# Moving x's block sums into the first MLP, emptying GpSimd in the second, and reordering VectorE and ScalarE within a pair

## The chip, the core and the metric

The kernel runs on one core of a Trainium2 chip. TensorE (PE) does the matrix products and writes PSUM; VectorE (DVE), ScalarE (ACT) and GpSimd (POOL) do the elementwise work; SyncE (SP) issues the DMAs between HBM and SBUF. Each engine works off its own queue in the order written and waits on semaphores of the others. The metric is the device time of one execution in microseconds. Before the change it is 1678.28 us, the median of three runs (1677.06 to 1678.48).

## The reference

Three stages run one after the other: an attention whose keys and values are first packed to 32 rows per head, an MLP with ELU, and an MLP with a rational activation. Everything is float32.

```python
p_packed = sm_attn(p, k, v)                    # 8 x 8 heads, 32 packed rows
out = sm_attn(q, p_packed, p_packed)           # 576 rows a head
x = out.transpose(0, 2, 1, 3).reshape(4608, 512)
h = x @ w_in;  x = where(h > 0, h, exp(min(h, 0)) - 1) @ w_out       # 512 -> 2048 -> 512
h = x @ w_in2
P = a[0] + a[1]*h + a[2]*h**2 + a[3]*h**3
Q = 1 + abs(b[0])*abs(h) + abs(b[1])*h**2
return (P / (Q + 1e-6)) @ w_out2
```

The inputs are scaled so that h is large, and the products need nearly full float32 precision. So every operand of a product is split into a high part (a cast to fp32r) and a low part (the value less its high part), and each product is three matmuls: high by high, high by low, low by high.

## The kernel before

**First MLP.** The attention of batch element b+1 and the first MLP of element b run interleaved, in 256 steps: 8 batch elements, 2 halves of 288 tokens, 16 tiles of 128 hidden features (`a_step`, L361). Step s issues six matmuls that make h of step s+2 (L382), ACT's exp and relu (L391, L392) and DVE's maximum (L397) for s+2, the high part on ACT (L402) and the low part on DVE (L407) for s+1, and twelve matmuls that add step s to the output in PSUM (L417). What else belongs to a step stands in four tables keyed by step: `ldq` (loads, run first), `peq` (attention matmuls), `cvq`, and `ewq` (other elementwise work, run after the step's own, L1222). At the end of a half, `a_evac` copies x, [128, 4, 288], from PSUM to SBUF, and `a_spill` (L447) writes it to the HBM tensor x2d with one DMA.

**Second MLP.** x @ w_in2 is done by the Strassen-Winograd scheme: x and w_in2 are cut into 2 by 2 blocks, and seven block products P1 to P7 replace eight. x's blocks are: two halves of the contraction by the two token halves of a batch element. Of x, the seven left operands are four blocks and four sums (t1 to t4), each with a high and a low part. The 2304 token columns are cut into 6 blocks of 384 (`TU`), the 16 hidden tiles into 8 pairs: 48 pairs in all. Per block, `x_load` brings x into two staging tiles, POOL makes the sums (`x_t`, L666), ACT the high parts (`x_hi`, L655) and POOL the low parts (`x_lo`, L660), during the pairs of the block before (for block 0, during the last steps of the first MLP).

Per pair and tile f (1 and 0) the activation is worked out from h: ACT makes Abs, Square and Identity (L701, L704, L707), DVE makes Q (L711) and two products `ta`, `tb` (L715, L719), ACT Ln and Exp (L722, L725) for the reciprocal, DVE two Newton steps `Na`, `Nb` (L729) and the result g (L733), ACT g's high part (L743), POOL its low part (L746). The second product takes 36 matmuls of 512 columns a pair (`out_mm`, L754) into six PSUM tiles, which are copied out at the end of each block (`out_ev`, L771).

**Order of a pair.** `window(s)` (L777) writes the three pairs in flight by hand: the products of pair s+2, the activation of s+1, the output of s. TensorE's order is P1, o0, P2, o1, P6, o2, P5, P7, o3, o4, P4, o5, P3, where P is six matmuls of 384 columns and o six of 512. All seven products go through one PSUM tile, `ab`, with two banks. Readers of it are ACT's copies s1, u2, u3 (`keep`, L692) and C21 (L867), and DVE's additions C12, C11, C22 (`c_add`, L695). The program orders every use of this tile behind the one written before it, on whichever engine and in whichever bank: P1, C12, s1, P2, C11, P6, u2, P5, P7, u3, C22, P4, C21, P3. Fourteen yields of windows -2 and -1 are pumped into the last steps of the first MLP (L1223).

Of the kernel before, what the change touches and what calls it, by code (L numbers as in the profile page):

```python
# [22 lines left out]
def packed_attention_moe_moe2_kernel(  # L23
# [399 lines left out]
    def a_evac(s):  # L423

        b, n, f, _ = a_step(s)
        if b == 0 and f < NF - 1:
# [3 lines left out]
        elif b == 0 and n == 1:  # L430
            x = mlp["x", s] = part[0][:, 1]
        elif b == B - 1:
            if n == 0:
                part[:] = [P.tile([128, 2, NKD, TA], F32, tag="v", name="xlast")]
            x = mlp["x", s] = part[0][:, n]
# [177 lines left out]
    P1, P2, P6, P5, P7, P4, P3 = range(7)  # L613

    swt, wo2, xs, stg, bst = {}, {}, [], {}, {}

    def s_load(p):
        for t in range(4):
            n = 2 if t < 3 else 1
            w = P.tile([128, n, 2, 2, 128], F32R, tag=f"wo{4 * (p % 2) + t}", name=f"sw_{p}_{t}")  # L620
            nc.sync.dma_start(out=w.bitcast(F32), in_=s2d[:, p % NPR, 2 * t:2 * t + n].bitcast(F32))
            swt[p, t] = w
# [11 lines left out]
    def x_slots(i):
        if i == 0:
            t = P.tile([128, 5, 2, 2, TU], F32R, tag="wi", name="xs_wi")
            xs.extend(t[:, k] for k in range(5))
        else:
            xs.append(P.tile([128, 2, 2, TU], F32R, tag=f"m{i - 1}", name=f"xs_m{i - 1}"))

    def x_stage():
        for tag in "kq":
            stg[tag] = P.tile([128, 3, 2, TU], F32, tag=tag, name=f"stage_{tag}")

    def x_load(n):
        u = slice(n * TU, (n + 1) * TU)
        for tag, k in (("k", 0), ("q", 2)):
            for i in range(2):
                nc.sync.dma_start(out=stg[tag][:, i], in_=x2d[:, k:k + 2, i, u])

    XSRC = (("k", 0), ("q", 0), ("k", 0), ("k", 2), ("k", 1), ("q", 0), ("q", 1))

    def x_hi(n, j):
        tag, i = XSRC[j]
        nc.scalar.copy(xslot(n, j)[:, 0], stg[tag][:, i])  # L655

    def x_lo(n, j):
        tag, i = XSRC[j]
        x = xslot(n, j)
        nc.gpsimd.tensor_tensor(x[:, 1], stg[tag][:, i], x[:, 0].bitcast(F32), ALU.subtract)  # L660

    def x_t(i):
        k, q = stg["k"], stg["q"]
        o, a, b = ((k[:, 2], k[:, 1], k[:, 0]), (k[:, 0], q[:, 1], k[:, 2]),
                   (k[:, 1], q[:, 1], k[:, 1]), (q[:, 0], q[:, 0], k[:, 0]))[i]
        nc.gpsimd.tensor_tensor(o, a, b, ALU.subtract)  # L666
# [623 lines left out]
```

## Time and profile before

| | |
|---|---|
| Median of three runs | 1678.28 us |
| Profiled execution | 1679.38 us |
| Its span, first to last instruction | 1677.6 us |
| TensorE busy | 1519.9 us (91%) |
| VectorE busy | 1226.6 us (73%) |
| ScalarE busy | 1080.7 us (64%) |
| GpSimd busy | 320.0 us (19%) |
| Mean granted clock of TensorE | 0.982 of full speed |
| Moved by DMA | 253.88 MB, 151 GB/s |

The time of the profiled execution is its span and 1.78 us around it. Busy time is the time in which an engine had an instruction running. TensorE's matmuls overlap and the ends of them are modelled, so the distance from one start to the next tells its pace, not the duration. The same holds for DVE and ACT in a smaller way: an instruction can start some hundredths of a microsecond before the one ahead of it is recorded as done. Two stages have to be kept apart: up to 717.1 us the first MLP alone, from 759.34 us the pairs of the second alone, with a mixture between.

### The profile page before, as it was taken

The page shows a single profiled execution, that of the slowest core. Times are in us where ns is not written, and L with a number is a line of the kernel's source. Part 1 is how long each engine was busy: PE and PEld are TensorE (multiplying, and loading weights), DVE is VectorE, ACT ScalarE, POOL GpSimd, SP SyncE. Part 2 cuts the span into 40 slices and gives each one's busy share as a digit, 9 for nine tenths or more (in the row PEclk, how much of TensorE's full clock was granted, in tenths as well). Part 3 has the DMA queues.
Part 4 walks back from the last instruction along what each step waited for, and adds up shares of the span by engine and source line. Part 5 has one row for each costly group of instructions (what it writes and reads, how often), then busy time and mean ns, then how long its engine had stood idle before and what let it go on. Part 6 is the DMA issues. An engine that isn't in the chain of part 4 may idle for free.

```text
span 1677.6 us, 26163 instructions
## 1 busy us (share of the span) xinstructions
PE 1519.9 (91%) x10194; PEld 1339.4 (80%) x10194; DVE 1226.6 (73%) x1826; ACT 1080.7 (64%) x1902; POOL 320.0 (19%) x170
## 2 busy tenths in 40 slices
PE   7899999999999999989888987888888888888987
PEld 5789899999999899987767866777777777777776
DVE  6886767666666667657777778677777787877776
ACT  4866666667676766566666666666656756665664
POOL 0000000000000000412442235233413432342221
PEclk9999999999999999999999999999999999999999
DMA  9533344444444323255544644654454446444531
GB/s 355 166 118 132 96 133 127 125 129 125 137 142 148 120 95 130 71 181 190 169 148 161 206 143 138 221 173 147 156 199 149 149 159 222 153 138 164 173 128 38
DMA packets 116490, 253.88 MB, mean 151 GB/s; under 512 B 9488, under 2 KB 55824, under 8 KB 114576
## 3 DMA queue, kind: packets, MB, share of 16 engines
q1 hardware_dynamic: 116368, 252.22, 46.0%
q8 instruction: 80, 1.31, 0.3%
q14 instruction: 42, 0.34, 0.1%
HBM read 210.24 MB, written 41.94 MB: 150 GB/s over the span
## 4 chain that ended last, share of the span: by engine, by line
PE 47%; DVE 36%; ACT 13%; issue 3%; DMA 1%; SPq 0%; DVEq 0%; ACTq 0%
PE acc L417 22%; PE h L382 11%; DVE w L729 10%; PE ab L677 8%; DVE t L733 6%; DVE t L719 5%; DVE t L715 4%; DVE w L711 3%; ACT A_all L743 3%; DVE h L695 3%; ACT w L701 2%; PE m L338 2%; ACT sq L704 2%; DVE stage_q L695 1%; PE acc L754 1%
## 5 line engine op out<-in xcount | busy, mean ns | idle before, releaser
L417 PE MATMUL acc<-gl_all,wo 128*128 128x288 f32 x3072 | 458.5, 298 | 8.9 <-DVE gl_all L407 5.6
L417 PEld LDWEIGHTS acc<-gl_all,wo 128*128 128x128 f32 x3072 | 419.0, 189 | 51.4 <-ACT g L392 22.6
L677 PE MATMUL ab<-xs_wi,sw 128*128 128x384 f32 x1200 | 248.6, 347 | 74.3 <-ACT h L867 31.1
L677 PEld LDWEIGHTS ab<-xs_wi,sw 128*128 128x128 f32 x1200 | 212.1, 191 | 110.3 <-ACT h L867 40.4
L382 PE MATMUL h<-A_all,m 128*128 128x288 f32 x1536 | 245.6, 295 | 2.1 <-DVE m L352 0.8
L729 DVE SCALAR_TENSOR_TENSOR w<-w,sq 128x768 f32<-128x768 f32 x192 | 224.9, 1172 | 0.0
L677 PE MATMUL ab<-xs_m,sw 128*128 128x384 f32 x816 | 173.5, 352 | 52.9 <-ACT h L867 29.9
L382 PEld LDWEIGHTS h<-A_all,m 128*128 128x128 f32 x1536 | 217.0, 188 | 3.9 <-DVE m L352 1.7
L677 PEld LDWEIGHTS ab<-xs_m,sw 128*128 128x128 f32 x816 | 147.7, 196 | 77.5 <-ACT h L867 39.9
L754 PE MATMUL acc<-wo,A_all 128*128 128x512 f32 x768 | 207.5, 398 | 0.0
L397 DVE SCALAR_TENSOR_TENSOR g<-g,h 128x288 f32<-128x288 f32 x256 | 115.8, 452 | 112.1 <-ACT g L392 111.9
L402 ACT CAST gl_all<-g 128x288 fp32r<-128x288 f32 x256 | 110.9, 433 | 131.2 <-PE acc L417 109.0
L407 DVE TENSOR_TENSOR gl_all<-g,gl_all 128x288 fp32r<-128x288 f32 x256 | 127.0, 496 | 78.6 <-ACT gl_all L402 77.6
L743 ACT CAST A_all<-t 128x768 fp32r<-128x768 f32 x72 | 60.2, 836 | 180.8 <-DVE t L733 180.8
L754 PEld LDWEIGHTS acc<-wo,A_all 128*128 128x128 f32 x768 | 144.7, 191 | 22.0
L746 POOL TENSOR_TENSOR A_all<-t,A_all 128x768 fp32r<-128x768 f32 x48 | 89.0, 1855 | 337.1 <-ACT A_all L743 264.8
L391 ACT ACTIVATE g<-h 128x288 f32<-128x288 f32 x256 | 105.2, 411 | 67.7 <-PE h L382 66.8
L666 POOL TENSOR_TENSOR stage_k<-stage_k 128x768 f32<-128x768 f32 x6 | 11.1, 1854 | 628.5 <-ACT g L391 628.5
L711 DVE SCALAR_TENSOR_TENSOR w<-sq,cf,w 128x768 f32<-128x768 f32 x96 | 109.1, 1137 | 18.3 <-ACT sq L704 17.7
L392 ACT ACTIVATE g<-g 128x288 f32<-128x288 f32 x256 | 113.8, 444 | 8.1
L733 DVE SCALAR_TENSOR_TENSOR t<-t,cf,w 128x768 f32<-128x768 f32 x96 | 114.1, 1188 | 3.4
L754 PE MATMUL acc_h<-wo,A_all 128*128 128x512 f32 x384 | 110.3, 411 | 2.2 <-ACT A_all L743 2.2
(417 smaller groups left out, 2105.6 us busy)
## 6 DMA issues: line engine op xcount, KB each, us to landing
sw<-s2d SPq DMA_DIRECT2D x144, 512.0 KB, 3.6
wo<-wo2d SPq DMA_DIRECT2D x96, 512.0 KB, 5.1
sw<-s2d SPq DMA_DIRECT2D x48, 256.0 KB, 2.7
...
```

The costliest lines, as they stand in the source:

```text
L382: nc.tensor.matmul(ps[:, :TA], lhsT=m[:, wx, r, c0:c0 + 128], rhs=A[:, ax, r, :], start=(i == 0), stop=(i == 5))
L392: nc.scalar.activation(d["e"], d["e"], AF.Relu, scale=-1.0, bias=1.0)
L397: nc.vector.scalar_tensor_tensor(d["g"], d["e"], -1.0, d["h"][:, :TA], ALU.mult, ALU.max)
L402: nc.scalar.copy(d["ghi"], d["g"])
L407: nc.vector.tensor_tensor(d["glo"], d["g"], d["ghi"].bitcast(F32), ALU.subtract)
L417: nc.tensor.matmul(acc[m][:, :TA], lhsT=w[:, wx, m * 128:(m + 1) * 128], rhs=d[g], start=(first and i == 0), stop=(last and i == 2))
L677: nc.tensor.matmul(m2["ab"][:, bank, :TU], lhsT=w[:, j % 2, wx, k, :], rhs=x[:, xx, k, :], start=(start and i == 0), stop=(i == 5), skip_g ...
L711: nc.vector.scalar_tensor_tensor(w, m2["sq", f], cf[:, 5:6], w, ALU.mult, ALU.add)
L729: nc.vector.scalar_tensor_tensor(w, w, c, m2["sq", f], ALU.add, ALU.mult)
L733: nc.vector.scalar_tensor_tensor(t, t, cf[:, 0:1], m2["w", f], ALU.add, ALU.mult)
L743: nc.scalar.copy(g_tile(p, f, 0), m2["t", f])
L754: nc.tensor.matmul(acc[i], lhsT=g_tile(p, f, g)[:, i * 128:(i + 1) * 128], rhs=w[:, wx, :], start=(p % NPR == 0 and f == 1 and k == 0), st ...
```

## The change

Three things change.

1. **x's sums and splits** are made in the first MLP, right after each half is evacuated (`x_prep`): four subtractions on DVE, seven casts on ACT and seven low parts on DVE, all on [128, 288], in eight pieces that the eight steps after the half take, one each, at the end of `ewq`. x2d now holds all seven operands, high and low: 14 DMAs a half, each of 147 KB in rows of 576 bytes, in place of one of 576 KB. The two token blocks are now the first and last 144 tokens of a half. In the second MLP `x_load` brings a finished operand with one DMA of 768 KB into one of 11 slots (9 before), seven a block. The last half's pieces fall into windows 0 to 3. The loads of v, k and q for later batch elements move by some steps.
2. **GpSimd** has no work left in the second MLP: g's low parts (`r_lo`) are DVE's.
3. **The order of a pair** is read from a table, `PLAN`, in which `+`, none, `-` and `=` stand for pairs s+2, s+1, s and s-1. TensorE's order stays as it was; of the uses of `ab`, C22 moves behind P4. On DVE and ACT the steps of the two tiles f are woven in another order, the weights of a product are loaded two pairs ahead, piece by piece behind the product that used them, and outputs are copied out on ACT alone.

```diff
+    PLAN = (
+        "P1+ C12 Id1 Q1 o0- s1+ ta1 Id0 P2+ S0+ Ln1 ta0 o1- Sq0 tb1 Abs0 C11+ P6+ Exp1 Q0 o2- u2+ Na1 Ln0 tb0 "
...
-    x2d = dram.tile([128, NKD, 2, NU], F32, tag="x2d", name="x2d")
+    x2d = dram.tile([128, 7, 2, 2, NU], F32R, tag="x2d", name="x2d")
...
-    def a_spill(s):
+    def x_prep(s):
         b, n, _, _ = a_step(s)
-        nc.sync.dma_start(out=x2d[:, :, n, b * TA:(b + 1) * TA], in_=mlp.pop(("x", s)))
+        x, sc = mlp.pop(("x", s))
...
+        def up(j):
+            hi[j] = tmp.pop(0)
+            nc.scalar.copy(hi[j].bitcast(F32R), src[j])
+        def low(j):
+            nc.vector.tensor_tensor(src[j].bitcast(F32R), src[j], hi[j], ALU.subtract)
+            for h, t in ((0, hi[j]), (1, src[j])):
+                nc.sync.dma_start(out=x2d[:, j, h, :, u].bitcast(F32), in_=t)
+            tmp.extend((hi[j], src[j]))
+        yield sub(t1, b12, b11), sub(t2, b22, t1), up(P1)
+        yield sub(b12, b22, b12), sub(t4, b21, t2), low(P1)
...
+            for js in ((P5, P7), (P2, P3, P6, P4)):
+                yield
+                for j in js:
+                    up(j)
+                yield
+                for j in js:
+                    low(j)
+                yield
...
-        i = (7 * n + j) % 9
+        i = (7 * n + j) % 11
...
+    def x_load(n, j):
+        if n >= NB2:
+            return
+        nc.sync.dma_start(out=xslot(n, j).bitcast(F32), in_=x2d[:, j, :, :, n * TU:(n + 1) * TU].bitcast(F32))
...
     def r_lo(p, f):
-        nc.gpsimd.tensor_tensor(g_tile(p, f, 1), m2["t", f], g_tile(p, f, 0).bitcast(F32), ALU.subtract)
+        nc.vector.tensor_tensor(g_tile(p, f, 1), m2["t", f], g_tile(p, f, 0).bitcast(F32), ALU.subtract)
...
+        plan = [(x.rstrip("+-="), s + {"+": 2, "-": 0, "=": -1}.get(x[-1], 1)) for x in PLAN]
+        if s == NPAIR - 3:
+            late = [x for x in plan if x[0] in ("o3", "o4", "o5")]
+            o2 = plan.index(("o2", s))
+            plan.insert(plan.index(("P5", s + 2)) + 1, ("o2", s))
+            del plan[o2]
+            plan = [x for x in plan if x not in late] + late
+        for name, p in plan:
+            if 0 <= p < NPAIR:
+                one(name, p)
+                if name[0] == "P":
+                    yield
...
-                at(ldq, end if b else 28, load_v, b + 2)
-                at(ldq, o + (20 if b else 26), load_k, b + 2)
-                at(ldq, o + NS + 3, load_q1, b + 2)
+                at(ldq, o + 28, load_v, b + 2)
+                at(ldq, o + (20 if b else 30), load_k, b + 2)
+                at(ldq, o + NS + 9, load_q1, b + 2)
...
-                at(ewq, s + 1, a_spill, s)
+                prep = x_prep(s)
+                for i in range(8):
+                    at(ewq, s + 1 + i, next, prep, None)
...
-        for s in range(NPAIR - 1):
+        for s in range(NPAIR):
             for _ in window(s):
                 pass
+            for i in range(2):
+                run(ewq, NA + 1 + 2 * s + i)
```

The first place is DVE's queue in a pair of the second MLP, from tile 1's g to the addition C11 of the next pair's products. Before: `t_8794` and `w_8792` belong to tile 1, `t_8797` and `w_8795` to tile 0; `h_8801` is tile 1's h, `stage_q` and `h_9190` are tile 0's in turn; `s_8798`, `u_8799`, `u_8800` are the copies s1, u2, u3.

```order
L733 SCALAR_TENSOR_TENSOR t_8794<-t_8794,cf,w_8792 128x768
L729 SCALAR_TENSOR_TENSOR w_8795<-w_8795,sq_8796 128x768
L695 TENSOR_TENSOR h_8801<-u_8800,ab 128x384
L729 SCALAR_TENSOR_TENSOR w_8795<-w_8795,sq_8796 128x768
L733 SCALAR_TENSOR_TENSOR t_8797<-t_8797,cf,w_8795 128x768
L695 TENSOR_TENSOR stage_q<-u_8799,ab 128x384
L711 SCALAR_TENSOR_TENSOR w_8792<-sq_8793,cf,w_8792 128x768
L715 TENSOR_TENSOR t_8794<-t_8794,h_8801 128x768
L711 SCALAR_TENSOR_TENSOR w_8795<-sq_8796,cf,w_8795 128x768
L695 TENSOR_TENSOR h_9190<-s_8798,ab 128x384
```

C22 (`h_8801<-u_8800`) stands here between the Newton steps of tile 0, and C12 (`stage_q<-u_8799`) follows tile 0's g directly.

In the changed kernel the same stretch; `t_9224` and `w_9222` are tile 1's, `t_9227` and `w_9225` tile 0's, `s_9228` holds s1 and later u3, `u_9229` holds u2.

```order
L759 SCALAR_TENSOR_TENSOR t_9224<-t_9224,cf,w_9222 128x768
L755 SCALAR_TENSOR_TENSOR w_9225<-w_9225,sq_9226 128x768
L759 SCALAR_TENSOR_TENSOR t_9227<-t_9227,cf,w_9225 128x768
L721 TENSOR_TENSOR h_9230<-s_9228,ab 128x384
L772 TENSOR_TENSOR A_all<-t_9224,A_all 128x768
L772 TENSOR_TENSOR A_all<-t_9227,A_all 128x768
L721 TENSOR_TENSOR h_9646<-u_9229,ab 128x384
L737 SCALAR_TENSOR_TENSOR w_9222<-sq_9223,cf,w_9222 128x768
L741 TENSOR_TENSOR t_9224<-t_9224,h_9230 128x768
L741 TENSOR_TENSOR t_9227<-t_9227,h_9646 128x768
L745 SCALAR_TENSOR_TENSOR t_9224<-t_9224,cf,h_9230 128x768
L721 TENSOR_TENSOR h_o<-s_9228,ab 128x384
```

C22 (`h_9230<-s_9228`) has moved behind both g, two low parts (L772) have come in, and between C12 (`h_9646<-u_9229`) and C11 (`h_o<-s_9228`) there stand four instructions of the activation: Q of tile 1, both `ta` and the `tb` of tile 1. Before, there were three: Q of both tiles and one `ta`.

The second place is DVE's queue in the first MLP, in the last of the eight steps after a half, up to the next low part of the step's own work. Before:

```order
L305 TENSOR_REDUCE s2m_1_2361<-s2x_1_2360 128x18
L306 TENSOR_SCALAR s2m_1_2361<-s2m_1_2361 128x18
L307 RECIPROCAL s2m_1_2361<-s2m_1_2361 128x18
L352 TENSOR_TENSOR m_1_2459<-m_1_2441,m_1_2459 128x1024
L407 TENSOR_TENSOR gl_all<-g_2451,gl_all 128x288
L397 SCALAR_TENSOR_TENSOR g_2482<-g_2482,h_2474 128x288
```

Between the low part of an attention weight product (L352) and the step's own low part nothing stands here.

In the changed kernel, with `x_47` the evacuated half:

```order
L310 TENSOR_REDUCE s2m_1_2429<-s2x_1_2428 128x18
L311 TENSOR_SCALAR s2m_1_2429<-s2m_1_2429 128x18
L312 RECIPROCAL s2m_1_2429<-s2m_1_2429 128x18
L357 TENSOR_TENSOR m_1_2537<-m_1_2519,m_1_2537 128x1024
L476 TENSOR_TENSOR x_47_2258<-x_47_2258 128x2x144 x2
L476 TENSOR_TENSOR x_47_2258<-x_47_2258 128x288 x2
L412 TENSOR_TENSOR gl_all<-g_2529,gl_all 128x288
L402 SCALAR_TENSOR_TENSOR g_2572<-g_2572,h_2564 128x288
```

Four low parts of x (L476) now stand ahead of the step's own low part (`gl_all`) and maximum.

## Rows read from the trace of the kernel before

**Rows 1.** Chain of waits of the page: share of the span by engine.

```profile
PE 47%; DVE 36%; ACT 13%; issue 3%; DMA 1%; SPq 0%; DVEq 0%; ACTq 0%
```

**Rows 2.** Windows: busy us (count) PE, PEld, DVE, ACT, POOL; PEclk; DMA share; GB/s.

```profile
497.00:584.00 87.00, 87.00 (x798) 79.97 (x797) 58.72 (x128) 58.46 (x135) 0.00 (x0) 1.00 0.41 144
...
759.30:776.20 16.90, 15.08 (x74) 12.82 (x72) 14.24 (x17) 9.18 (x13) 2.15 (x2) 1.00 0.81 295
...
1224.00:1381.00 157.00, 135.71 (x624) 116.04 (x624) 120.77 (x126) 100.82 (x138) 52.83 (x28) 0.96 0.52 168
```

**Rows 3.** Timeline, TensorE in one pair: start, us, what xcount [idle <-releaser].

```profile
1107.90 1.21 PE L677 MATMUL ab<-xs_m,sw 128*128 128x384 f32 x6
...
1111.09 1.31 PE L677 MATMUL ab<-xs_m,sw 128*128 128x384 f32 x6 [0.59 <-ACT s L692]
...
1112.24 1.55 PE L754 MATMUL acc_h<-wo,A_all 128*128 128x512 f32 x6
...
1117.11 1.20 PE L677 MATMUL ab<-xs_wi,sw 128*128 128x384 f32 x6
1118.14 2.93 PE L754 MATMUL acc<-wo,A_all 128*128 128x512 f32 x12
...
1120.91 1.21 PE L677 MATMUL ab<-xs_wi,sw 128*128 128x384 f32 x6
```

**Rows 4.** Timeline, VectorE and GpSimd in the same pair.

```profile
1109.14 0.56 DVE L695 TENSOR_TENSOR h<-u,ab 128x384 f32<-128x384 f32 x1 [3.71 <-PE ab L677]
...
1111.82 1.02 DVE L711 SCALAR_TENSOR_TENSOR w<-sq,cf,w 128x768 f32<-128x768 f32 x1
...
1112.75 0.55 DVE L695 TENSOR_TENSOR stage_q<-s,ab 128x384 f32<-128x384 f32 x1
...
1113.21 0.95 DVE L715 TENSOR_TENSOR t<-t,h 128x768 f32<-128x768 f32 x1
...
1114.08 1.01 DVE L719 SCALAR_TENSOR_TENSOR t<-t,cf,h 128x768 f32<-128x768 f32 x1
...
1119.82 1.85 POOL L746 TENSOR_TENSOR g_v<-t,A_all 128x768 fp32r<-128x768 f32 x1 [9.74 <-ACT A_all L743]
...
1120.57 1.93 DVE L729 SCALAR_TENSOR_TENSOR w<-w,sq 128x768 f32<-128x768 f32 x1
```

**Rows 5.** Timeline, ScalarE in the same pair.

```profile
1106.71 0.94 ACT L701 ACTIVATE w<-h,ab_sb 128x768 f32<-128x768 f32 x1
...
1107.56 0.83 ACT L704 ACTIVATE sq<-h 128x768 f32<-128x768 f32 x1
...
1108.29 1.02 ACT L707 ACTIVATE t<-h,cf 128x768 f32<-128x768 f32 x1
...
1110.58 0.46 ACT L692 COPY s<-ab 128x384 f32<-128x384 f32 x1
```

**Rows 6.** Waits over the whole run: engine line <- whom: us, times, longest.

```profile
PE ab L677 <- ACT s L692: 38.0, 48, 2.9
```

**Rows 7.** Timeline, TensorE: the first pair loop window, and the last with products.

```profile
759.34 1.23 PE L677 MATMUL ab<-xs_wi,sw 128*128 128x384 f32 x6
...
1630.02 2.37 PE L677 MATMUL ab<-xs_m,sw 128*128 128x384 f32 x12 [1.32 <-ACT h L867]
```

**Rows 8.** Lines, VectorE, one batch element of the first MLP (497 to 584 us).

```profile
L397 DVE SCALAR_TENSOR_TENSOR g<-g,h 128x288 f32<-128x288 f32 x32 | 14.5, 454 | 15.4 <-ACT g L392 15.4
L407 DVE TENSOR_TENSOR gl_all<-g,gl_all 128x288 fp32r<-128x288 f32 x32 | 14.5, 453 | 10.4 <-ACT gl_all L402 10.3
```

**Rows 9.** Timeline, end of the first MLP, VectorE and TensorE.

```profile
671.41 1.81 DVE L407 TENSOR_TENSOR gl_all<-g,gl_all 128x288 fp32r<-128x288 f32 x1 [0.67 <-ACT gl_all L402]
...
682.40 1.87 PE L417 MATMUL acc<-gl_all,wo 128*128 128x288 f32 x11 [3.46 <-DVE gl_all L407]
```

**Rows 10.** DMA issues by line (KB, us to landing); then weight writes, line L604.

```profile
stage_k<-x2d SPq DMA_DIRECT2D x12, 384.0 KB, 7.1
...
DMA to landing us min/median/max: 2.0/2.3/6.4
```

More of the change, by code (lines that the diff above doesn't have):

```diff
@@ L429, in a_evac @@
             x = part[0][:, n]
[L430 to L435, printed above, removed]
-        else:
-            x = mlp["x", s] = P.tile([128, NKD, TA], F32, tag="kq"[n], name=f"x2_{s}")
+        else:
+            if b == 0 and n == 1:
+                x, sc = part[0][:, 1], part[0][:, 0]
+            else:
+                t = P.tile([128, 2 * NKD, TA], F32, tag="kq"[n] if n or b in (0, B - 1) else "v", name=f"x2_{s}")
+                x, sc = t[:, :NKD], t[:, NKD:]
+            sc = [sc[:, i] for i in range(NKD)]
+            if b == 0 and n == 0:
+                sc += [part[0][:, 0, i] for i in range(NKD)]
+            mlp["x", s] = x, sc
         for m in range(NKD):
@@ L612, in packed_attention_moe_moe2_kernel, with s_load @@
     NA = B * 2 * NF
[L613 to L622, printed above, removed]
+    swt, wo2, xs, bst = {}, {}, {}, {}
+    def s_load(p, t):
+        if p >= NPAIR:
+            return
+        n = 2 if t < 3 else 1
+        w = P.tile([128, n, 2, 2, 128], F32R, tag=f"wo{4 * (p % 2) + t}", name=f"sw_{p}_{t}")
+        nc.sync.dma_start(out=w.bitcast(F32), in_=s2d[:, p % NPR, 2 * t:2 * t + n].bitcast(F32))
+        swt[p, t] = w
     def wo2_load(p):
@@ L630, in xslot @@
     def xslot(n, j):
-        i = (7 * n + j) % 9
-        return xs[i]
[L634 to L666, printed above, removed]
+        i = (7 * n + j) % 11
+        if i not in xs:
+            if i < 5:
+                t = P.tile([128, 5, 2, 2, TU], F32R, tag="wi", name="xs_wi")
+                xs.update((k, t[:, k]) for k in range(5))
+            elif i == 9:
+                xs[9] = m2["k"][:, :4 * TU].rearrange("p (h k t) -> p h k t", h=2, k=2)
+            else:
+                xs[i] = P.tile([128, 2, 2, TU], F32R, tag=f"m{i - 5}" if i < 9 else "q", name=f"xs_{i}")
+        return xs[i]
+    def x_load(n, j):
+        if n >= NB2:
+            return
+        nc.sync.dma_start(out=xslot(n, j).bitcast(F32), in_=x2d[:, j, :, :, n * TU:(n + 1) * TU].bitcast(F32))
     m2 = {}
@@ L766, in out_ev @@
         while u < end:
-            e = min(end, (u // TA + 1) * TA)
+            e = min(end, (u // TR + 1) * TR)
             segs.append((u, e))
@@ new lines, in packed_attention_moe_moe2_kernel, with one @@
+    BANK = dict(P1=(0, True), P2=(1, True), P6=(0, False), P5=(1, True), P7=(0, False), P4=(0, False), P3=(1, False))
+    SUMS = dict(C11=(0, 0, "s1"), C12=(0, 1, "u2"), C22=(1, 1, "s1"))
+    JS = dict(P1=P1, P2=P2, P6=P6, P5=P5, P7=P7, P4=P4, P3=P3)
+    def one(name, p):
+        op, i = name[:-1], int(name[-1])
+        if op == "P":
+            prod(p, JS[name], *BANK[name])
+            n, k = divmod(p, NPR)
+            if k == NPR - 1 and JS[name] < 3:
+                x_load(n + 1, JS[name] + 4)
+        elif op == "S":
+            s_load(p + 2, i)
+        elif op == "o":
+            if p < NPAIR - 1:
+                out_mm(p, i)
+        elif op == "e":
+            if p % NPR == NPR - 1 and p < NPAIR - 1:
+                out_ev(p, i, nc.scalar)
+        elif name in SUMS:
+            c_add(p, *SUMS[name])
+        elif name in ("s1", "u2", "u3"):
+            keep("u2" if name == "u2" else "s1")
+        elif name == "C21":
+            nc.scalar.copy(h_tiles(p)[1][:, 0], m2["ab"][:, 0, :TU])
+        else:
+            dict(Abs=lambda: r_abs(p, i), Sq=lambda: r_sq(p, i), Id=lambda: r_id(p, i), Q=lambda: r_q(i),
+                 ta=lambda: r_ta(p, i), tb=lambda: r_tb(p, i), Ln=lambda: r_ln(i), Exp=lambda: r_exp(i),
+                 Na=lambda: r_n(i, 1.0 + 1e-6), Nb=lambda: r_n(i, -2.0), g=lambda: r_g(i),
+                 hi=lambda: r_hi(p, i), lo=lambda: r_lo(p, i))[op]()
```

185 lines of the change are left out of this document (47 added, 138 removed).

## The prediction

> **What bounds the kernel now.** I read the chain of waits first, then the windows by stage, then one pair on three engines. The chain is split: TensorE has 47% of it, VectorE 36%, ScalarE 13% [rows 1]. A kernel that one engine bounds throughout does not look so; the windows show why [rows 2]. In the first MLP (497 to 584 us, one batch element) TensorE is busy for all of 87.00 us, DVE for 58.72 and ACT for 58.46. There only TensorE counts, and elementwise work fits beside it. In the second MLP (1224 to 1381 us, one block of eight pairs) TensorE is busy 135.71 of 157 us, and POOL works too. A pair takes 157 / 8 = 19.6 us there. Between the first P1 of the pair loop and the last (759.34, and 1630.02 plus the 1.16 that P3 takes ahead of P1) lie 45 pairs and 871.8 us, 19.37 us each [rows 7].
>
> What would TensorE need? Unhindered, P takes 1.03 us (1117.11 to 1118.14) and o 2.77 / 2 = 1.385 us (1118.14 to 1120.91) [rows 3]. Seven P and six o, with 1.04 for P: 7.28 + 8.31 = 15.59 us. So 3.8 us a pair are lost. Two losses can be seen. First, the tile `ab` hands over from engine to engine: C12 on DVE starts at 1109.14, just after P1 ends at 1107.90 + 1.21, though it needs only P3 [rows 3, 4], and P2 waits until s1 ends at 1110.58 + 0.46 [rows 3, 5]; this wait comes 48 times, 38.0 us [rows 6]. Second, a DVE instruction that meets a POOL one takes twice its time: `Nb` at 1120.57 took 1.93 us beside POOL's low part (1119.82 to 1121.67) [rows 4], against 0.95 to 1.02 for its like.
>
> **The change, part by part.**
>
> *DVE in a pair.* POOL's two low parts go, and with them the doubled durations. Two low parts of 768 columns come to DVE. The trace has no such row; the subtraction's nearest kin is `ta`, two inputs from SBUF at the same width, 0.95 us [rows 4], and I take that (bounds: 0.87 as a start-to-start distance, 1.02 as Q). Consecutive instructions start up to 0.08 us before the end of the one ahead (1113.21 + 0.95 against 1114.08) [rows 4]. So DVE needs 3 additions x 0.48, Q and g 4 x 0.94, `ta` 2 x 0.87, `tb` 2 x 0.93, four Newton steps and two low parts 6 x 0.87: 14.0 us a pair. That is below TensorE's 15.59.
>
> The Trainium skill (VectorE: DVE Perf Modes, "The DRAIN you can't avoid") says that the next op does not start until the pipe is empty; by it the overlap of 0.08 would not exist, and 17 instructions would need 15.4 us. The rows contradict it where the next instruction does not need the last one's result. I keep 14.0; a DVE without overlap is a rival below, with the durations of the rows.
>
> *ACT in a pair.* The same 16 instructions, in other order: about 11.6 us. It does not bound by its sum.
>
> *The order of a pair.* I set P1's start at 0 and lay out the queues. P1 ends at 1.21, C12 starts at 1.24. s1 on ACT comes behind C12 and Id1 and ends near 2.5, so P2 starts at 2.57 where o0 would have let it at 2.43. DVE goes on from C12 with Q1, ta1, ta0, tb1 and only then C11: 1.24 + 0.48 + 0.94 + 0.87 + 0.87 + 0.93 = 5.33, and C11 ends at 5.92 with 0.56 and the hand-over. `ta0` needs Id0, which follows s1: 2.46 + 1.02 = 3.48, just before DVE is there at 3.53. P6 waits for C11, so it starts at 5.92; TensorE alone would be there at 2 x 1.04 + 2 x 1.385 = 4.85. From P6 on nothing is late: u2 ends near 7.6 and P5 comes at 8.34; u3 ends at 11.1 and P4 comes at 13.19; C22 and C21 after P4 end at 15.5 and P3 comes at 15.62; the last low part ends at 17.2, 0.5 us into the next pair and before o0 wants it. From P6 to the next P1 it is 5 x 1.04 + 4 x 1.385 = 10.74. The pair: 5.92 + 10.74 = 16.66 us. A P behind a wait took 1.15 (1111.09 to 1112.24) and not 1.04 [rows 3]; P2 and P6 wait, so I add 0.2: **16.85 us**, against 19.37. The ring through ACT (C21, high part of tile 0, Abs, Square, Id1, s1, Id0; rows of 0.46 to 1.02 us [rows 5]) arrives within 0.1 us of the same point, so whatever ACT loses adds as well.
>
> 45 pairs: 758 us in place of 871.8. The last half's x pieces lie in windows 0 to 3: five instructions' worth of DVE time in the first and four casts or low parts in later ones, of which 1 us a window is not covered: +4.
>
> *x's sums and splits.* Per half, DVE gets 4 subtractions and 7 low parts of 288 columns, 453 ns by the kin row L407 [rows 8], 0.37 start to start: 11 x 0.37 = 4.1 us; ACT 7 casts, about 2.5 us. Two halves a batch element: DVE goes from 58.7 to about 67, ACT to 64, of 87 us [rows 2]. By the sum it is hidden. If nothing were hidden, 16 x (4.1 + 2.5) = 106 us would come on; if all is, 0. The truth is near the hidden end, since TensorE never idled there. But the last piece of each half puts four low parts, 1.5 us, ahead of the step's own (the order shows it); DVE idles ahead of L397 and L407 for 25.8 us over 32 steps, 0.8 a step [rows 8], so 0.7 us overflows; 15 halves make 10. Four casts also wait until the buffers they overwrite have landed in x2d, two steps (5.4 us) after the writes; weight writes of this kind land in 2.3 us but up to 6.4 [rows 10]: +2. On the other side POOL's work leaves the end of this stage, where a low part took 1.81 us and TensorE stood for 3.46 [rows 9]: -4. Net +8.
>
> *Transfers.* The stage loads go, 24 x 384 KB [rows 10], 1.6 MB a block; 7 x 786 KB = 5.5 MB come. A block moved 168 GB/s x 157 us = 26.4 MB, and now 30.3 MB in 8 x 16.85 = 135 us, 225 GB/s. The window at 759 us carried 295 GB/s at 0.81 [rows 2]. Cost nothing; weights are asked for two pairs ahead, which hides landing times.
>
> *The end.* From the last P1 (1631.2) to the end (1677.6) it is 46.4 us. Two low parts of 0.95 replace two of 1.85, and a DVE instruction doubled beside them loses its 0.95 or so [rows 4]: -3, to 43.
>
> **Sum.** 759.34 + 8 = 767; + 758 + 4 + 43 = 1572 us of span. The profiled execution took 1.8 us more than its span, and 1.1 us more than the median; that gives **1573 us**.
>
> **Rivals.**
> - *TensorE's floor.* If C11 is in time (ACT or DVE faster than laid out), a pair takes 15.6 to 15.9: 1517 to 1531 us. The row for P2's wait speaks against it: the chain through `ab` already costs now. Chance 0.12.
> - *DVE without overlap.* Every DVE instruction costs its full duration, 14.0 + 17 x 0.08 = 15.4 us a pair, and the six from C12 to C11 cost 0.5 us more: 17.35 us a pair, 45 x 0.5 = 22 us in all, 1595 us. For it: dependent instructions stand back to back in places (Nb, g). Against: the starts at 1113.21 and 1114.08. Chance 0.18; the Trainium skill's DRAIN rule, named above, is this case.
> - *The first MLP pays.* ACT is held at casts behind writes that queue behind a 1 MB load of k, 3 us at each of 15 halves in place of the 12 us in my sum: +33, 1606 us. For it: landing up to 6.4 us; against: two steps of room. Chance 0.10.
> - *Slower: the queues carry no more.* If the 168 GB/s of a block are what these transfers can get, a block of 30.3 MB takes 180 us, products wait for x, and 45 pairs take 1014: 1829 us. It decides from 155 us a block on (196 GB/s). The 295 GB/s row speaks against it. Chance 0.04.
>
> **How the numbers follow.** The forecast has 0.56. Its own bounds: 16.4 to 17.3 us a pair (45 x 0.45 = 20 us up or down), the first MLP -5 to +25, the end 40 to 47. With the DVE rival inside and the floor and the slower case left out, the range is 1538 to 1610. What can be told from no change is 0.2%, some 3.4 us; every case but the last lies far beyond. Faster 0.95, the same 0.01, slower 0.04.
>
> **What the profile would show.** POOL idle after the start; no DVE row of 768 columns near 1.9 us; P1 to P1 near 16.85, with P6 waiting about 1 us for DVE's C11 in every pair and P2 hardly; lows on DVE of 0.95; the first P1 of the pair loop near 767 us. Wrong it would be if P6 does not wait (the floor), if P2 waits for s1 longer than P6 for C11 (ACT is the ring), if the pair loop starts past 785 us, or if products wait for DMA.

## The result and the profile after

The changed kernel takes 1622.44 us (median of four runs, 1621.8 to 1624.08) against 1678.38; the ratio is 0.9666, 95% interval 0.965 to 0.9683. It is 3.3% faster where 6.3% were forecast, and 49 us above the predicted 1573, outside the range of 1538 to 1610.

The page's chain of waits, share of the span by engine (answers to [rows 1]):

```profile
PE 66%; DVE 21%; ACT 7%; issue 3%; DMA 2%; SPq 0%; DVEq 0%; ACTq 0%
```

Windows by stage, columns as in [rows 2]: one batch element of the first MLP, the part where the first MLP and the first two pairs are woven together, the pair loop, the end.

```profile
525.00:614.00 89.00, 87.33 (x794) 79.65 (x793) 66.36 (x150) 61.08 (x146) 0.00 (x0) 1.00 0.51 164
...
745.00:811.20 66.20, 46.38 (x246) 43.60 (x245) 22.94 (x40) 26.86 (x52) 0.00 (x0) 0.85 0.54 177
811.20:1576.60 765.40, 726.62 (x3513) 623.31 (x3512) 651.90 (x779) 546.51 (x757) 0.00 (x0) 1.00 0.66 216
1576.60:1620.00 43.40, 34.82 (x151) 28.42 (x149) 30.01 (x36) 23.49 (x32) 0.00 (x0) 0.95 0.19 61
```

The pair loop takes 765.4 us, 17.0 a pair (871.8 before), as forecast; its granted clock is 1.00, where it was 0.97. The end takes 43.4, also as forecast. The surprise stands in the first column: the pair loop starts at 811.2 us, where 767 was forecast and it had been 759.3 [rows 7]; anything past 785 was named as a sign of being wrong. In the woven part TensorE is busy for 46 of 66 us, and its granted clock is 0.85.

The same chain edge in the pair, timeline of TensorE, DVE and ACT (answers to [rows 3 to 5]):

```profile
1101.65 1.31 PE L703 MATMUL ab<-xg_k,sw 128*128 128x384 f32 x6
...
1102.81 1.20 PE L703 MATMUL ab<-xs_wi,sw 128*128 128x384 f32 x6
...
1104.04 0.56 DVE L721 TENSOR_TENSOR h_o<-u,ab 128x384 f32<-128x384 f32 x1 [0.72 <-PE ab L703]
...
1105.24 1.31 PE L703 MATMUL ab<-xs_wi,sw 128*128 128x384 f32 x6
1105.44 0.95 DVE L741 TENSOR_TENSOR t<-t,h 128x768 f32<-128x768 f32 x1
...
1106.31 0.95 DVE L741 TENSOR_TENSOR t<-t,h_o 128x768 f32<-128x768 f32 x1
...
1107.18 1.01 DVE L745 SCALAR_TENSOR_TENSOR t<-t,cf,h 128x768 f32<-128x768 f32 x1
...
1108.11 0.54 DVE L721 TENSOR_TENSOR h<-s,ab 128x384 f32<-128x384 f32 x1
...
1108.71 1.31 PE L703 MATMUL ab<-xs,sw 128*128 128x384 f32 x6 [0.78 <-DVE h L721]
...
1118.56 1.31 PE L703 MATMUL ab<-xg_k,sw 128*128 128x384 f32 x6
```

P3 to P3 is 1118.56 - 1101.65 = 16.91 us. C12 starts right behind P1, ta1, ta0 and tb1 follow, C11 starts at 1108.11 behind tb1, and P6 waits for it. The two ta start 0.87 apart and take 0.95: the overlap is there again.

Waits of TensorE over the run, us in total, times, longest (answers to [rows 6]); C11's sum writes h and h_o by turns:

```profile
PE ab L703 <- DVE h_o L721: 21.6, 24, 3.4
PE ab L703 <- DVE h L721: 20.2, 24, 2.2
PE acc L422 <- DVE gl_all L412: 16.2, 13, 3.3
```

**Where the 52 us of the first MLP were lost.** DVE's instruction that makes g comes once in each step (L397 before, L402 after), so its starts show the drift step by step (us from the start of the span):

| step | before | after | after less before |
|---|---|---|---|
| 36 | 144.1 | 152.5 | +8.4 |
| 120 | 372.7 | 394.7 | +22.0 |
| 249 | 723.5 | 752.1 | +28.6 |
| 255 | 754.0 | 799.8 | +45.8 |
| first P1 of the pair loop | 759.3 | 811.2 | +51.9 |

Three places. *At step 33* the score product of batch element 2 waits for k. TensorE and SyncE after:

```profile
146.04 1.22 PE L178 MATMUL s1h<-k,p 64*32 64x288 f32 x16 [6.60 <-DMA k<-in_kT_dram]
147.18 3.25 PE L422 MATMUL acc<-gl_all,wo 128*128 128x288 f32 x12
...
131.34 6.45 SPq L478 DMA_DIRECT2D x2d<-x  x5
...
140.75 0.35 SPq L105 DMA_DIRECT2D k<-in_kT_dram  x1
```

The first half's x lies in k's buffer while it is split. k's load (step 30, where it was 26) goes out at 140.75, behind the split's writes in SyncE's queue; before, at 119.35. Behind the wait the twelve matmuls take 3.25 us, at a granted clock of 0.50 from 146 to 151 us, where they take 1.74 at a clock of 1.00.

*In the steps of the splits*, +20 us from step 36 to 249. One of these steps on DVE, first before, then after (start, us, row):

```profile
287.38 0.46 DVE L397 SCALAR_TENSOR_TENSOR g<-g,h 128x288 f32<-128x288 f32 x1 [0.46 <-ACT g L392]
287.75 0.75 DVE L305 TENSOR_REDUCE s2m<-s2x 128x18 f32<-128x576 f32 x1
...
288.93 1.16 DVE L352 TENSOR_TENSOR m<-m,m 128x1024 fp32r<-128x1024 f32 x1
...
290.45 0.69 DVE L493 SCALAR_TENSOR_TENSOR w2('i', 0, 3)_cb<-raw1('i', 0, 3)_3352,w2('i', 0, 3)_cb 128x512 uint32<-128x512 uint32 x1
291.06 0.45 DVE L407 TENSOR_TENSOR gl_all<-g,gl_all 128x288 fp32r<-128x288 f32 x1
```

```profile
304.11 0.46 DVE L412 TENSOR_TENSOR gl_all<-g,gl_all 128x288 fp32r<-128x288 f32 x1 [4.31 <-ACT gl_all L407]
...
304.90 0.45 DVE L402 SCALAR_TENSOR_TENSOR g<-g,h 128x288 f32<-128x288 f32 x1 [0.33 <-ACT g L397]
...
307.97 0.69 DVE L541 SCALAR_TENSOR_TENSOR w2('i', 0, 3)_cb<-raw1('i', 0, 3)_3480,w2('i', 0, 3)_cb 128x512 uint32<-128x512 uint32 x1
308.58 1.56 DVE L476 TENSOR_TENSOR x<-x 128x288 fp32r<-128x288 f32 x4
310.05 0.45 DVE L412 TENSOR_TENSOR gl_all<-g,gl_all 128x288 fp32r<-128x288 f32 x1
```

Before, DVE has no idle time at all between 287.38 and 291.06: the attention's sums, m's low part and two w2 pieces fill the step. After, four low parts stand behind them, and the step's own low part (L412) starts 5.15 us behind the g at the head of the step, where it was 3.68 (287.38 to 291.06). DVE also comes to that step late: ahead of it, it stands 4.31 us for ACT's high part (L407), which follows the casts of x, and one of those waits 1.12 us for a buffer to land. TensorE then stands 3.33 us:

```profile
303.31 0.43 ACT L473 CAST x<-x 128x288 fp32r<-128x288 f32 x1 [1.12 <-DMA x2d<-x]
...
310.56 2.28 PE L422 MATMUL acc<-gl_all,wo 128*128 128x288 f32 x11 [3.33 <-DVE gl_all L412]
```

*In the woven part*, +23 us from step 249 on. TensorE there after:

```profile
773.81 1.34 PE L703 MATMUL ab<-xs,sw 128*128 128x384 f32 x6 [2.44 <-ACT h L825]
...
776.02 1.74 PE L422 MATMUL acc<-gl_all,wo 128*128 128x288 f32 x12
...
780.99 1.31 PE L703 MATMUL ab<-xs_wi,sw 128*128 128x384 f32 x6 [2.44 <-ACT s L718]
```

Of the fourteen P in this part, six wait 2.2 to 3.4 us and three more 1.3 to 1.6 us for an evacuation of `ab` that ACT or DVE is given just before it. (An evacuation is the copy or sum that reads the product out of PSUM.) The loop that weaves the two stages calls `next(mix)` in a step, which runs `window` up to its next `yield`. Before, a piece was a product and then the elementwise work behind it; with the table, a piece ends *with* the product. So a P follows directly on the copy that it waits for, and the step's twelve matmuls `acc` stand behind it.

### The profile page after: what moved, and what is told of

The parts are those of the page before. It is cut to its first block, busy times and chain, and to the rows that moved or that the text cites. A ratio compares the mean times of both kernels' runs of the same rounds, so it can differ in the third digit from the quotient of the medians.

```text
span 1620.0 us, 26751 instructions
## 1 busy us (share of the span) xinstructions
PE 1511.1 (93%) x10194; PEld 1331.3 (82%) x10194; DVE 1248.4 (77%) x2078; ACT 1087.5 (67%) x1992; POOL 3.3 (0%) x8
## 4 chain that ended last, share of the span: by engine, by line
PE 66%; DVE 21%; ACT 7%; issue 3%; DMA 2%; SPq 0%; DVEq 0%; ACTq 0%
PE ab L703 20%; PE acc L422 18%; PE acc L778 16%; PE h L387 9%; DVE t L741 5%; DVE t L745 3%; DVE h L721 2%; DVE h_o L721 1%; PE m L343 1%; ACT g L397 1%; ACT g L396 1%; DVE g L402 1%; DVE x L476 1%; ACT gl_all L407 1%; DMA x2d<-x 1%
## 5 line engine op out<-in xcount | busy, mean ns | idle before, releaser
L422 PE MATMUL acc<-gl_all,wo 128*128 128x288 f32 x3072 | 466.5, 300 | 20.3 <-DVE gl_all L412 16.2
L703 PE MATMUL ab<-xs_wi,sw 128*128 128x384 f32 x960 | 202.3, 349 | 33.0 <-DVE h_o L721 12.2
L703 PEld LDWEIGHTS ab<-xs_wi,sw 128*128 128x128 f32 x960 | 168.4, 191 | 60.8 <-DVE h_o L721 17.3
L407 ACT CAST gl_all<-g 128x288 fp32r<-128x288 f32 x256 | 110.9, 433 | 156.4 <-PE acc L422 93.2
L703 PE MATMUL ab<-xs,sw 128*128 128x384 f32 x912 | 187.0, 344 | 22.5 <-DVE h L721 6.3
L412 DVE TENSOR_TENSOR gl_all<-g,gl_all 128x288 fp32r<-128x288 f32 x256 | 116.2, 454 | 111.8 <-ACT gl_all L407 110.8
L703 PEld LDWEIGHTS ab<-xs,sw 128*128 128x128 f32 x912 | 158.2, 188 | 45.4 <-ACT h L825 12.8
L755 DVE SCALAR_TENSOR_TENSOR w<-w,sq 128x768 f32<-128x768 f32 x192 | 182.7, 952 | 5.8
L402 DVE SCALAR_TENSOR_TENSOR g<-g,h 128x288 f32<-128x288 f32 x256 | 115.6, 451 | 86.3 <-ACT g L397 86.1
L397 ACT ACTIVATE g<-g 128x288 f32<-128x288 f32 x256 | 113.8, 445 | 8.1
L825 ACT COPY h<-ab 128x384 f32<-128x384 f32 x48 | 23.1, 481 | 128.1 <-DVE h L721 128.1
L759 DVE SCALAR_TENSOR_TENSOR t<-t,cf,w 128x768 f32<-128x768 f32 x96 | 97.6, 1017 | 1.7
L737 DVE SCALAR_TENSOR_TENSOR w<-sq,cf,w 128x768 f32<-128x768 f32 x96 | 97.0, 1011 | 0.2 <-ACT w L727 0.2
L751 ACT ACTIVATE sq<-sq,cf 128x768 f32<-128x768 f32 x96 | 89.7, 935 | 1.6
L748 ACT ACTIVATE sq<-w,cf 128x768 f32<-128x768 f32 x96 | 89.8, 935 | 0.5 <-DVE w L737 0.5
```

The source lines that it names most:

```text
L397: nc.scalar.activation(d["e"], d["e"], AF.Relu, scale=-1.0, bias=1.0)
L402: nc.vector.scalar_tensor_tensor(d["g"], d["e"], -1.0, d["h"][:, :TA], ALU.mult, ALU.max)
L407: nc.scalar.copy(d["ghi"], d["g"])
L412: nc.vector.tensor_tensor(d["glo"], d["g"], d["ghi"].bitcast(F32), ALU.subtract)
L422: nc.tensor.matmul(acc[m][:, :TA], lhsT=w[:, wx, m * 128:(m + 1) * 128], rhs=d[g], start=(first and i == 0), stop=(last and i == 2))
L703: nc.tensor.matmul(m2["ab"][:, bank, :TU], lhsT=w[:, j % 2, wx, k, :], rhs=x[:, xx, k, :], start=(start and i == 0), stop=(i == 5), skip_g ...
```

## The experiments

Medians in us; the ratio is to the kernel before, with its 95% interval; "pair" is the median distance of C21's copy from one pair to the next, "start" the first P1 of the pair loop.

| run | median | ratio | pair | start |
|---|---|---|---|---|
| after | 1622.44 | 0.9666 (0.965 to 0.9683) | 16.91 | 811.2 |
| e1_mix_yield | 1597.88 | 0.9516 (0.9502 to 0.953) | 16.93 | 788.1 |
| e2_k_use_later | 1617.85 | 0.9639 (0.9623 to 0.9655) | 16.93 | 808.2 |
| e3_no_splits | 1581.68 | 0.9423 (0.9407 to 0.9438) | 16.91 | 774.9 |
| e12_no_lows | 1602.7 | 0.9546 (0.9528 to 0.9563) | 16.93 | 790.3 |
| e5_spread | 1610.3 | 0.9589 (0.9573 to 0.9606) | 16.94 | 799.0 |
| e4_c11_early | 1574.65 | 0.9378 (0.9363 to 0.9393) | 15.98 | 807.9 |
| e6_low_on_pool | 1622.71 | 0.9666 (0.9651 to 0.968) | 16.90 | 814.0 |
| e7_old_order | 1694.76 | 1.0095 (1.008 to 1.011) | 18.47 | 812.5 |
| e8_c11_yield | 1555.41 | 0.9264 (0.9251 to 0.9278) | 16.00 | 786.5 |
| e9_three | 1541.02 | 0.9177 (0.9165 to 0.919) | 15.99 | 773.1 |
| e10_four | 1539.35 | 0.9173 (0.916 to 0.9185) | 15.99 | 775.5 |
| e11_c11_two | 1532.07 | 0.9125 (0.9113 to 0.9138) | 15.86 | 771.7 |

**The woven part: e1_mix_yield.**

```diff
+                if name[0] == "P" and (name, p) != ("P1", 0):
+                    yield
                 one(name, p)
-                if name[0] == "P":
-                    yield
...
-                next(mix)
+                next(mix, None)
```

> The kernel after, but where the first MLP and the first two pairs are woven together, a piece of a pair now begins with its product P and ends ahead of the next one, in place of ending with a P. So the step's own 18 matmuls stand between a P and the evacuation that the next P waits for. Theory A (the pieces are cut in the wrong place: a P stands right behind the sum or copy that it waits for, with nothing to run meanwhile): the six waits of 1.3 to 3.4 us ahead of P between 745 and 806 us go, and the half clock behind them; the first P1 of the pair loop comes 15 to 24 us earlier than 811.21, at 787 to 796, and the time falls to 1598 to 1607 us. Theory B (DVE and ACT are full there, with low parts and x's splits ahead of the step's own work): the waits move to gl_all and h, P1 stays within 3 us of 811, and the time is 1619 to 1625 us.

Theory A, with 24.6 us. The same products stand in the same steps, only on the other side of the yield. The part takes 43 us, TensorE stands for 5.6 us of it where it stood for 19.8, and its granted clock is back at 0.96; timeline and window of this run, then the window of the same part in the kernel before:

```profile
759.02 1.21 PE L703 MATMUL ab<-xs,sw 128*128 128x384 f32 x6
760.07 1.74 PE L422 MATMUL acc<-gl_all,wo 128*128 128x288 f32 x12
...
762.44 1.21 PE L703 MATMUL ab<-xs,sw 128*128 128x384 f32 x6
```

```profile
745.00:788.00 43.00, 37.44 (x241) 36.45 (x241) 23.80 (x40) 26.28 (x52) 0.00 (x0) 0.96 0.75 257
```

```profile
717.00:757.00 40.00, 35.13 (x231) 33.71 (x231) 24.48 (x34) 25.18 (x47) 5.64 (x3) 1.00 0.51 172
```

DVE and ACT do the same work in 43 us (23.80 and 26.28 us busy) as after did in 66 (22.94 and 26.86), so they were not full.

**x's splits: e3_no_splits, e12_no_lows, e5_spread.** In e3 the pieces keep only their DMAs; in e12 one line goes:

```diff
         def low(j):
-            nc.vector.tensor_tensor(src[j].bitcast(F32R), src[j], hi[j], ALU.subtract)
```

> The kernel after without the elementwise work on x: the differences, the casts and the low parts of all 16 halves are left out, and unsplit blocks of x are written to the same places by the same number of DMAs in the same steps. Theory A (the +20 us that steps 36 to 249 lost, some 1.45 us a half, are the elementwise bursts): the first P1 of the pair loop comes some 20 us earlier, near 791, the first four windows give about 4 us more, and the time is 1596 to 1602 us; the wait for k at step 33 and the waits in the mixture stay. Theory B (the loss comes from the writes and loads of x, which are 786 KB more a block and stay here): P1 stays past 805 us and the time at 1613 us or more.

> The kernel after without the seven low parts of each half of x: the differences and the seven casts stay, and the unsplit block is written in the low part's place. Leaving out all the elementwise work took 40.8 us off, halving the bursts of low parts 12.1 us. Theory A (VectorE's bursts are the whole loss, ACT's casts are covered): the pair loop starts 25 to 36 us earlier than 811.21 and the time is 1582 to 1597 us. Theory B (ACT's casts, four in a step of their own, cost as much as the low parts): the start comes 10 to 20 us earlier, the time is 1600 to 1612 us.

e3 leaves out the differences, casts and low parts, to measure what they cost. It gives more than either theory: 40.8 us, of which 36.4 come before the pair loop and 4.2 in it. My expectation that the wait for k would stay was wrong: without casts and low parts the writes go out early, k is asked for at 128.43, and step 36 starts at 143.7. So of the 21.4 us by which k's load moved, 9.1 are the four steps, which cost nothing, and 12.3 the writes ahead of it. From step 36 to step 249 after takes 25.0 us more than e3, so that is what the elementwise work costs: some 1.8 us for each of 14 halves. In the same steps e3, with step 249 at 718.3, gains 4.8 us on before. Up to step 230 the two stay within 0.7 us of each other at all steps but two, so the writes and loads cost nothing that shows; the gain comes between steps 230 and 238, where GpSimd's work lay [rows 9], forecast as 4.

In e12, which writes the unsplit blocks, the low parts are worth 19.7 us of the 40.8, so the other half is left for casts and differences (and k behind them): theory B, its start 0.9 us past the edge. From step 36 to 249 e12 takes 584.3 us, e3 574.6 and after 599.6: low parts 15.3 us, casts and differences 9.7, the latter by subtraction only. TensorE's waits for the step's own low part came to 16.2 us in after (shown above); here they are in e12 and then in e5:

```profile
PE acc L422 <- DVE gl_all L412: 7.2, 6, 1.8
```

```profile
PE acc L422 <- DVE gl_all L412: 5.4, 5, 1.8
```

e5 has all the work, in nine steps:

```diff
-            for js in ((P5, P7), (P2, P3, P6, P4)):
-                yield
-                for j in js:
-                    up(j)
-                yield
-                for j in js:
-                    low(j)
-                yield
+            yield
+            yield up(P5), up(P7)
+            yield low(P5)
+            yield low(P7)
+            yield up(P2), up(P3)
+            yield low(P2), low(P3), up(P6), up(P4)
+            yield low(P6), low(P4)
...
-                for i in range(8):
+                for i in range(9):
```

> The kernel after with the same elementwise work for x's splits, in nine steps behind a half in place of eight: at most two low parts in one step where there were four, and the casts ahead of them in turn. Leaving the work out altogether brought the pair loop forward by 36.4 us, of which 8.8 were the wait for k and the rest some 1.8 us a half. Theory A (the loss is four low parts, 1.56 us, in a step whose VectorE queue is full already): the pair loop starts 10 to 18 us earlier than 811.21, and the time is 1604 to 1613 us. Theory B (it is the number of instructions that counts, wherever they stand): the start moves by less than 4 us and the time is 1618 to 1624 us.

Theory A: 12.1 us, about half of the 25, by the spacing alone (of casts as well as low parts). The other 13 are spread over the halves, and no run tells them apart further.

**k: e2_k_use_later and e10_four.**

```diff
-                s1s, s2s, ms = (1, 3, 6, 7, 9), (13, 20), (18, 23, 26, 30)
+                s1s, s2s, ms = (1, 3, 6, 7, 9) if b > 1 else (4, 5, 7, 8, 9), (13, 20), (18, 23, 26, 30)
```

> The kernel after, but for the one batch element whose k is loaded behind x's first split (batch element 2), the two score products that read k come at steps 36 and 37 in place of 33 and 35. Theory A (the k load waits for the split's writes and is late by 6.6 us, and the clock falls behind that wait): the wait goes, step 36 comes 8 us earlier, and what was gained is kept: 1613 to 1616 us. Theory B (TensorE would lose it anyway: DVE and ACT are behind by as much, from the splits of that half): another wait takes its place within the next ten steps and the time stays at 1620 to 1624 us.

The wait is gone and step 36 comes 9.5 us earlier, but by step 40 all but 4.0 are given back; 4.6 us in all, a time between the two theories. TensorE in e2, where ACT's part is late twice:

```profile
148.73 2.21 PE L422 MATMUL acc<-gl_all,wo 128*128 128x288 f32 x12 [1.37 <-ACT gl_all L407]
...
154.10 0.72 PE L178 MATMUL s1h<-k,p 64*32 64x288 f32 x16 [2.37 <-ACT E L202]
```

I took the second for a fault of my spacing and tried two steps' distance (4, 6, 8, 9, 10), on top of the other edits:

> As the three edits together, and for batch element 2 the two score products that read k come at steps 36 and 38 in place of 33 and 35, two steps apart as they were (one step apart, at 36 and 37, the second waited 2.4 us for the exponentials of the first, and 4.6 of 9.5 us were kept). Theory A (the late k costs what its wait shows and the clock behind it): 7 to 9 us less than with three edits. Theory B (the splits of the half behind it hold ACT and DVE up there anyway): at most 5 us less.

Theory B. Against e9 the gain is 1.7 us, inside the intervals; the first row of e10's stall:

```profile
149.99 3.25 PE L422 MATMUL acc<-gl_all,wo 128*128 128x288 f32 x12 [2.21 <-ACT gl_all L407]
```

In steps 32 to 40 ACT has the second half's casts and the exponentials. By these rows ACT caught up in the 6.6 us at k; without that wait it is waited for. The profile names the wait that ends last, not the only one. How much of the 8.4 us the late k costs by itself stays open: 4.6 us in after, 1.7 on top of the other edits.

**The pair: e4_c11_early.**

```diff
-        "P1+ C12 Id1 Q1 o0- s1+ ta1 Id0 P2+ S0+ Ln1 ta0 o1- Sq0 tb1 Abs0 C11+ P6+ Exp1 Q0 o2- u2+ Na1 Ln0 tb0 "
+        "P1+ C12 Id1 Q1 o0- s1+ ta1 Id0 P2+ S0+ Ln1 ta0 C11+ o1- Sq0 tb1 Abs0 P6+ Exp1 Q0 o2- u2+ Na1 Ln0 tb0 "
```

> The kernel after with one word of the order moved: DVE's sum C11 ahead of tb1 in place of behind it. Theory A (the predicted ring: C11 is late behind ta0 and tb1, and P6 waits 0.78 us for it in each pair): the wait ahead of P6 goes, the rest of DVE's queue comes 0.5 us later where nobody waits, a pair takes 15.8 to 16.1 us in place of 16.91, and the time is 1573 to 1588 us. Theory B (the ring through ACT, C21 to s1, is late by the same amount, as worked out to 0.1 us): a wait ahead of P2 or P3 grows instead, a pair takes 16.6 us or more, and the time is 1608 us or more.

Theory A, with 47.8 us for one word. The pair in e4, DVE and TensorE:

```profile
1099.71 1.21 PE L703 MATMUL ab<-xs_wi,sw 128*128 128x384 f32 x6
...
1102.36 1.82 DVE L741 TENSOR_TENSOR t<-t,h 128x768 f32<-128x768 f32 x2
...
1104.09 0.54 DVE L721 TENSOR_TENSOR h_o<-s,ab 128x384 f32<-128x384 f32 x1
...
1104.69 1.33 PE L703 MATMUL ab<-xs,sw 128*128 128x384 f32 x6
```

P6 starts 1104.69 - 1099.71 = 4.98 us after P1, where it took 1108.71 - 1102.81 = 5.90. So C11's place behind tb1 set the pair, as forecast.

**Engine or order: e6_low_on_pool and e7_old_order.** e6 is after with `r_lo` back on `nc.gpsimd`; e7 is after with the table rewritten to the order of before:

```diff
-        "P1+ C12 Id1 Q1 o0- s1+ ta1 Id0 P2+ S0+ Ln1 ta0 o1- Sq0 tb1 Abs0 C11+ P6+ Exp1 Q0 o2- u2+ Na1 Ln0 tb0 "
+        "P1+ C12 Abs0 s1+ Sq0 Id0 Q1 ta1 Q0 o0- P2+ S0+ C11+ Ln1 Exp1 ta0 tb1 o1- P6+ Ln0 u2+ Exp0 Na1 tb0 Nb1 g1 "
...
+        "o2- P5+ S1+ P7+ e4= e0- hi1 lo1 Na0 e5= u3+ C22+ Nb0 e2- e1- g0 o3- o4- e3- P4+ S2+ hi0 lo0 C21+ o5- P3+ S3+ "
+        "Abs1+ Sq1+ Id1+")
```

> The kernel after with the two low parts of a pair back on GpSimd, as before: the new order alone, with x's splits in the first MLP. Theory A (an instruction of VectorE with two inputs that meets one of GpSimd takes twice its time, so GpSimd gains nothing): VectorE rows near 1.9 us come back behind each low part, and a pair takes 17.2 us or more: 1633 us or more. Theory B (the order is all: P6 waits for C11, which stands far from the low parts, and VectorE has 1.7 us less to do): a pair takes 16.6 to 16.9 us, 1608 to 1622 us.

> The kernel after with the order of a pair's work put back to that of before (Abs and Square of tile 0 behind C12, both Ln and Exp early, the low parts right behind their high parts, Abs, Square and Id of tile 1 at the pair's end), but with the low parts on VectorE: the change of engine alone. Theory A (the order carries the gain: by my layout VectorE stands behind each high part, and s1 comes late behind Abs): a pair takes 18.0 to 18.8 us, so 50 to 85 us more than after: 1672 to 1707 us. Theory B (taking GpSimd's contention away carries it): 16.9 to 17.5 us a pair, at most 1650 us.

e6 runs like after to 0.3 us: theory B, at the far end of its range, so the DVE time that it spares is worth nothing here. e7 is 72 us slower than after: theory A. Its pair loop takes 834.3 us (812.5 to 1646.8), against 765.4 in after and 871.8 before. So of the 106.4 us that the pair loop gained, the order carries 68.9. The other 37.5 came with the rest of the change (sums and splits out of the pairs, weights loaded piece by piece, low parts off GpSimd), and no run takes these apart; in the new order taking GpSimd out adds nothing. e7 is slower than before because its pair loop starts 53 us later. Its rows show what the old order does with low parts on DVE:

```profile
1162.05 1.31 PE L703 MATMUL ab<-xs,sw 128*128 128x384 f32 x6 [0.99 <-DVE h L721]
...
1164.82 0.96 DVE L772 TENSOR_TENSOR g<-t,xg_k 128x768 fp32r<-128x768 f32 x1 [0.90 <-ACT xg_k L769]
...
1169.55 1.31 PE L703 MATMUL ab<-xs_wi,sw 128*128 128x384 f32 x6 [0.59 <-ACT s L718]
```

DVE stands 0.90 us at each low part until ACT has made the high part; C22 comes late to P4, and s1 to P2.

**Together: e8, e9, e11.**

> The two edits together that brought 24.6 us (the pieces of the woven part begin with their P) and 47.8 us (C11 ahead of tb1). If their places are apart, the gains add: 1550 us, with 15.98 us a pair and the pair loop from about 787 us on. If the earlier start of the pair loop only moves a wait for x's or the weights' loads into its first windows, less than half of the first gain is left: 1562 us or more.

> Three edits together: the woven part's pieces begin with their P, C11 stands ahead of tb1, and the splits take nine steps with at most two low parts in each. The first two together measured 1555.41 us, the third alone took 12.1 us off. If the third loss lies in the first MLP ahead of the woven part, as I hold, the gains add: 1541 to 1545 us, with the pair loop from about 775 us on. If part of it was the woven part's own slowness, which the first edit has cured already, it is 1547 us or more.

> As the four edits together, but C11 goes one place further ahead, in front of ta0. By my layout C11 then starts as soon as P2 has ended, P6 waits for nothing, and what is left are the 0.28 us ahead of P2 and of P3: 15.8 to 15.95 us a pair in place of 15.98, 2 to 8 us less in all. If VectorE has to wait for P2 there, everything behind comes later, and the pair takes 16.0 to 16.3: the same or up to 15 us more.

e8's median lies 5 us above the sum of the two gains, nearer to 1550 than to 1562. In the profiled runs the spans add up to 2.1 us (1620.0 less 23.8 and 45.6 makes 1550.6, for 1552.7), of which 1.7 is the start: e4's edit alone had brought it forward by 3.3 us, and beside e1's 1.6 of that is left. e9 adds e5's edit, with 14.4 us, so this gain adds in full. e11 has the four edits and C11 one place further ahead (part of the table's first line, against e10):

```diff
...
- ta1 Id0 P2+ S0+ Ln1 ta0 C11+ o1- Sq0 tb1
+ ta1 Id0 P2+ S0+ Ln1 C11+ ta0 o1- Sq0 tb1
...
```

It is the fastest: 1532.07 us, 7.3 below e10 as forecast, 5.6% below after and 8.8% below before. TensorE is busy for 714.5 of the 716.3 us from 771.7 to 1488.0, its pair loop, so the order has next to nothing left to gain there.

## Why the prediction was wrong in size

**Right:** the pair. The ring P1, C12, Q1, two ta, tb1, C11, P6 was laid out at 16.66 and taken as 16.85; it measures 16.91, and e4 shows that this very link sets it. 45 pairs and the last half's pieces took 765.4 us for 762; e3, without those pieces, is 4.2 shorter there, for the 4 foreseen. P6 waited 0.78 for the 1 us foreseen. No product waits for x, so the queue rival fell. DVE's overlap held: the ta rows overlap by 0.08, and the pair did not take the 17.35 of the rival without it. The Trainium skill (VectorE: DVE Perf Modes, "The DRAIN you can't avoid") says that the next op does not start until the pipe is empty, and adds that one that is not held starts earlier; the prediction left the addition out and saw a contradiction. The rows agree with the addition: the two ta, neither of which needs the other, overlap, while tile 0's g starts 0.04 us after the end of the Newton step that it needs (1114.19 + 0.95, and 1115.18).

The prediction named P2's wait as the loss at `ab`. The largest one before was another, P3's for C21's copy:

```profile
PE ab L677 <- ACT h L867: 61.0, 43, 2.7
```

In after it comes to 6.1 us in 4 times. The layout had P3 free of it, so the number did not suffer.

**Right by luck:** the end, 43.4 us for 43. The 3 us were put on the low parts of GpSimd and the DVE instructions beside them. With the low parts back on GpSimd (e6) the end takes 43.6; with them on DVE in the old order (e7) 46.9, where before took 46.4. So moving the low parts is not what shortened the end; e7 points to the order.

**Wrong:** the first MLP, +52 for +8, with -5 to +25 as its bounds. This is the term of the sum that failed, in three steps.

1. *The overflow of 10 and the 2 for casts* were mis-sized: the splits cost 25.0 us (after against e3, steps 36 to 249). For the low parts I set four of them against an average idle time of 0.8 us a step, but the step shown above has none; they cost 15.3 there (after against e12). The casts, four in one step, had 2 us; with the differences they are left with 9.7.
2. *The transfers* were weighed for the second MLP and put at nothing; left out was that k's load moves behind the split's writes, with k wanted three steps later: 8.4 us up to step 36, 6.6 of them the wait. The rival "the first MLP pays" had a load of k in it, but the other way round, and put 3 us on each half. One wait came, not fifteen; the casts wait 3.6 us for landings in the whole run. It gave 1606, the nearest number to the result, by a mechanism that is not the one.
3. *The woven part* was not in the sum at all. I read the new table for the pair loop, where `yield` has no effect, and not for the steps in which it decides what lies between a P and the evacuation it waits for. e1 puts it at 23.1 us.

By stage: 8.4 (up to step 36) + 25.0 (splits, steps 36 to 249) - 4.8 (GpSimd's share, e3 against before in the same steps) + 23.1 (the place of the yield) = 51.7 of the 51.9 measured. The -4 for GpSimd's share was right, as far as e3 shows it.

One claim about before is not shown. The prediction named GpSimd's doubling of DVE's instructions as a loss of the pair; e6 has GpSimd back in the new order and loses nothing. Whether it cost the pair anything in the old order, no run shows.
